# A fused retention and bilinear FFN kernel: two loads moved behind a group's transposing DMAs, and one early stretch of attention work moved eight products later

## The chip, the cores and the metric

The kernel runs on one core of one Trainium2 chip. The metric is device time in microseconds (us); the kernel before has a median of 329.77 us in three runs (328.47 to 330.15).

## What is computed

q, k and v are float32 of shape (8 batches, 8 heads, 576 positions, 64). Cut to what matters:

```python
scores = matmul(q, k.transpose(0, 1, 3, 2)) / sqrt(64)
Dmat   = where(i >= j, gamma[h] ** (i - j), 0)        # gamma[h] = 1 - 2 ** (-5 - h)
attn   = matmul(scores * Dmat, v)                     # no softmax
x      = attn.transpose(0, 2, 1, 3).reshape(4608, 512)
out    = ((x @ w_a) * (x @ w_b)) @ w_out              # 512 -> 1536 -> 512, float32 out
```

Because the mask is a power of a distance and there is no softmax, attention can be done block by block: a block of 64 positions takes the scores inside itself, and everything earlier through a running 64x64 sum of k times v, the state.

## The kernel before

**FFN.** The 4608 tokens go through the FFN in ten blocks of 512, 256, 256 and then seven times 512 tokens. In a block, w_a and w_b are taken in 12 chunks of 128 columns: four products `pa` (TensorE, summed in PSUM), a cast `ha` by ScalarE, four products `pb`, and a multiplication `hT` by VectorE. Then for every 128 tokens twelve products `po` give an output tile, which ScalarE (even tiles) or VectorE (odd tiles) copies to `osb` and SyncE's queue (SP) stores. All of these products are issued at line 466. They share a PSUM pool of four buffers.

**Attention.** The tokens come in 18 groups of 256, numbered from 0. Groups 0 to 2 are made ahead of the others, in six steps. Each group n from 3 on goes through:

1. `load_pair(n)` (L148): six loads by SP of 256 KB each, two for each of q, k, v, into float32 tiles with four buffers for each of the three.
2. `ahead(n)` (L481 to L486): POOL casts q and k to `qkb` in six instructions and scales v to `vb` in one.
3. `turn(n)` (L514): two transposing DMAs by SP, `qkb` to `qkT`, q first and then k.
4. `stretch(n, n - 1)`: 128 small matmuls on TensorE, in four sets of 32: the outputs of group n - 1 from the states (L638), the new sums of group n (L548), the scores of group n (L610), the outputs of group n - 1 from the keys (L651). Group 5's outputs are not in a stretch: `open_alone(5)` does the first set and `close_outputs(5)` the last.
5. What follows for VectorE and ScalarE (adding sums, casting states, masking scores, scaling the output into the FFN's input `xT`) is put in a list `later`. FFN code takes one piece of it at certain points, in a 256-token block once after each chunk and at three places and the end of an output tile.

**Order of the work.** A list `todo`, written by hand, holds (position, function, arguments). The position counts products of the FFN (512 columns wide; one of 256 columns counts a half). The FFN generator runs through its blocks and, at the end of a chunk or of every fourth `po`, runs what is due. Each engine executes its own instructions in the order in which they are issued, so the list sets the order on every engine's queue, on SP's and POOL's too. Around the change: block 2 (tokens 768 to 1023) lies at positions 216 to 288, its `po` from 264; block 3 at 288 to 432, block 4 at 432 to 576. `load_pair(9)` and `load_pair(10)` stand at 345.1 and 345.2, `ahead(9)` at 390, `turn(9)` at 422, stretch (9, 8) at 460, `ahead(10)` at 462, `turn(10)` at 494, stretch (10, 9) at 532. `turn(n)` for n from 9 on ends with `load_pair(n + 2)`. SP runs well behind these positions in the first half of the kernel, since the transfers are slower than the list.

**Early waits.** From group 6 on, `wait_early` makes FFN products ahead of a stretch wait for what the stretch needs: the seventh before it for the scaled v, the sixth for the transposed q, the third for the transposed k (L468 to L472).

**Buffers that bind around the change.** `qkb`, `vb` and `qkT` have three buffers each, the sums and states two, the PSUM tiles for scores and for outputs one. A stretch of its own block takes two of the four FFN buffers for `kv` until VectorE has added both halves.

Of the kernel before, what the change touches and what calls it, by code (L numbers as in the profile page):

```python
# [18 lines left out]
def kernel(  # L19
# [44 lines left out]
    def rows_of(n):  # L64

        if n not in LEFT:
            b, m = PAIRS[n]
            return [(kp, 0, 128, b, 256 * m + 128 * kp) for kp in (0, 1)]
        return [(i // 2, 64 * (i % 2), 64, 4 * LEFT[n] + i, S - 64)
                for i in range(4)]  # L70
# [69 lines left out]
    def load_pair(n, which=(0, 1, 2)):  # L140
        if n >= NP:
            return
        paired.setdefault(n, {})
        for i in which:
            name, src = (("qf", q), ("kf", k), ("vf", v))[i]
            t = stage.tile([128, 2 * DM], FP32, tag=name, name=name + "2")
            for kp, r0, m, b, s0 in rows_of(n):
                nc.sync.dma_start(  # L148
                    t[r0:r0 + m, kp * DM:(kp + 1) * DM]
                    .rearrange("p (h d) -> p h d", h=H),  # L150
                    src[b, :, s0:s0 + m, :].rearrange("h s d -> s h d"))
            paired[n][i] = t
# [13 lines left out]
    Q, K, V = 0, 1, 2  # L166
# [342 lines left out]
    def turn(n):  # L509
        qkb = of(natural, n)[0]  # L510
        qkT = qkt_pool.tile([128, 2, 2, HP, 128], BF16, tag="qkT",
                            name="qkT2")
        for w in (0, 1):
            ready[n].append(nc.sync.dma_start_transpose(  # L514
                qkT[:, w].rearrange("p k c s -> p (k c) s"), qkb[:, w]))
        transposed[FIRST + n, "pair"] = qkT
        if n >= 9:
            load_pair(n + 2)

    def of(store, n):  # L520
        return store[FIRST + n, "pair"]
# [402 lines left out]
    def turn_step(i):  # L924
# [3 lines left out]
    todo = [(100, early_casts, ()), (112, turn_step, (4,)),  # L928
            (112.1, cast_step, (5, Q, "act")), (116, score_step, (4,)), (116, state_step, (4,)),
            (124, turn_step, (5,)), (128, output_step, (4,)),  # L930
            (128, score_step, (5,)), (128, state_step, (5,)),
            (140, output_step, (5,))]
# [1 line left out]
    todo += [(136, total_of, (2,))]  # L934
    todo += [(28 + 6 * step, pair_tables, (step,)) for step in range(13)]
    todo += [(170, stretch, (3, None)), (197, stretch, (4, 3)),
             (232, stretch, (5, 4)), (266, open_alone, (5,)),
             (270, close_outputs, (5,)), (336, stretch, (6, None)),
             (372, stretch, (7, 6)), (408, stretch, (8, 7))]
    for n in range(8, NP, 2):  # L940
        todo += [(starts[n] - 116, stretch, (n + 1, n)),
# [4 lines left out]
    placed = {args[0]: at for at, fn, args in todo if fn is stretch}  # L946
    casts = {3: 116, 4: 116, 5: 141, 6: 200, 7: 250, 8: 330}
    turns = {4: 116, 5: 145, 6: 240, 7: 338, 8: 345}
    loads = {7: 212, 8: 271, 9: 345.1, 10: 345.2}
    todo += [(145.1, load_pair, (6, (K,))),  # L950
             (145.2, load_pair, (6, (Q,))), (145.3, load_pair, (6, (V,)))]
    for n in range(9, NP):
        casts[n], turns[n] = placed[n] - 70, placed[n] - 38
# [1 line left out]
    for fn, places in ((ahead, casts), (turn, turns), (load_pair, loads)):  # L955
        todo += [(at, fn, (n,)) for n, at in places.items()]
# [45 lines left out]
```

## Time and profile before

| | us |
|---|---|
| median of three runs | 329.77 (328.47 to 330.15) |
| the profiled execution | 332.06 |
| its span, first to last instruction | 330.3 |
| TensorE busy in the span | 322.0 |
| VectorE, ScalarE, POOL busy | 161.9, 129.2, 116.6 |
| mean granted TensorE clock | 0.995 |
| bytes moved | 50.37 MB, 152 GB/s over the span |
| stretch (5, 4) on TensorE | 73.97 to 75.50 |
| outputs of group 5: opened, closed | 84.17, 85.52 |
| first product of block 3 | 89.36 |
| stretches (7, 6), (8, 7), (9, 8), (10, 9) begin | 109.19, 117.44, 133.34, 150.48 |

An entry of a timeline gives start and length in us, the engine, the line and the operation, the tiles (out<-in), the shape, the count of instructions merged, and in brackets how long the engine sat idle before it and what ended that. PE is TensorE's matmul queue, PEld its weight loads, SPq SyncE's DMA issues: an issue's length is the time that SP spends on it, and the data lands later. The first half of the kernel also brings in the weights and most of q, k and v.

### The profile page before, as it was taken

Reading aid. Unit: us, or ns where it says so; the run is one execution under the profiler, and the core shown is the slowest. Engines: PE = TensorE matmul, PEld = TensorE weight load, DVE = VectorE, ACT = ScalarE, POOL = GpSimd, SP = SyncE. Lnnn points to the kernel's source line nnn. Section 1 sums busy time; section 2 is a strip of 40 time slices with the busy share of each in tenths; the row PEclk is TensorE's granted clock in tenths of the full one; section 3 lists DMA queues with packets and bytes.
Section 4 is the critical chain, followed back from the end, with each engine's and each line's share of the span. In section 5 each row is a group of like instructions: output and inputs, shape, how many; then the busy total and the mean of one; then the engine's idle time right before and its main releaser. Section 6 shows DMA issues by size and latency. Waiting matters only on the chain.

```text
span 330.3 us, 8653 instructions
## 1 busy us (share of the span) xinstructions
PE 322.0 (97%) x3615; PEld 166.3 (50%) x3615; DVE 161.9 (49%) x289; ACT 129.2 (39%) x286; POOL 116.6 (35%) x150
## 2 busy tenths in 40 slices
PE   7899999999999997999999999999999999999996
PEld 3564458778444553545454545454445444444443
DVE  5744454667246753656165625662456246414321
ACT  6745754464335532343235312532332333213321
POOL 3890068640957086554063405360420000000000
PEclk9999999999999999799999999999999999999999
DMA  7999999999999999991699158945850420031013
GB/s 218 250 175 207 251 234 212 204 188 211 226 223 213 203 197 227 232 223 52 158 209 223 50 133 191 214 84 147 180 113 2 136 58 0 2 95 32 3 25 102
DMA packets 143175, 50.37 MB, mean 152 GB/s; under 512 B 124576, under 2 KB 138656, under 8 KB 143136
## 3 DMA queue, kind: packets, MB, share of 16 engines
q1 hardware_dynamic: 138384, 45.10, 65.3%
q0 software_dynamic: 4752, 4.72, 8.9%
q8 instruction: 28, 0.46, 0.6%
q14 instruction: 11, 0.09, 0.1%
HBM read 37.75 MB, written 9.44 MB: 143 GB/s over the span
## 4 chain that ended last, share of the span: by engine, by line
PE 78%; SPq 9%; DMA 8%; POOL 2%; issue 1%; ACT 1%; DVE 0%; POOLq 0%; ACTq 0%; DVEq 0%
PE po L466 24%; PE pb L466 24%; PE pa L466 23%; SPq L148 5%; DMA vf<-in_v_dram 5%; SPq L159 2%; DMA qf<-in_q_dram 2%; PE o L638 1%; PE o L651 1%; DMA qkT<-qkb 1%; POOL qkb L485 1%; PE sc L610 1%; PE kv L548 1%; SPq L514 1%; PE pa L738 1%
## 5 line engine op out<-in xcount | busy, mean ns | idle before, releaser
L779 DVE TENSOR_TENSOR hT<-ha,pb 128x512 bf16<-128x512 bf16 (+1 forms) x120 | 75.7, 633 | 101.7 <-PE pb L466 94.9
L768 ACT CAST ha<-pa 128x512 bf16<-128x512 f32 (+1 forms) x120 | 64.6, 542 | 121.9 <-PE pa L466 118.7
L466 PE MATMUL pb<-xT,wb_sb 128*128 128x512 bf16 (+1 forms) x480 | 111.8, 358 | 0.2
L466 PE MATMUL pa<-xT,wa_sb 128*128 128x512 bf16 (+1 forms) x468 | 109.5, 359 | 1.8 <-DMA qkT<-qkb 1.8
L466 PE MATMUL po<-wo_sb,hT 128*128 128x512 bf16 (+2 forms) x444 | 97.5, 374 | 0.0
L466 PEld LDWEIGHTS <-wb_sb 128*128 128x128 bf16 x480 | 46.9, 98 | 47.0 <-DMA qkT<-qkb 0.8
L466 PEld LDWEIGHTS <-wa_sb 128*128 128x128 bf16 x468 | 44.9, 98 | 46.7 <-DMA qkT<-qkb 2.3
L466 PEld LDWEIGHTS <-hT 128*128 128x128 bf16 x444 | 41.9, 98 | 47.3
L481 POOL CAST qkb<-qf 64x1024 bf16<-64x1024 f32 x15 | 15.5, 1030 | 85.0 <-DMA qf<-in_q_dram 72.9
L486 POOL TENSOR_TENSOR vb<-vf,vs 128x1024 bf16<-128x1024 f32 x15 | 28.5, 1902 | 12.6 <-PE o L651 4.4
L804 DVE COPY osb<-po 128x512 f32<-128x512 f32 (+1 forms) x16 | 10.9, 683 | 39.6 <-PE po L466 39.6
L802 ACT COPY osb<-po 128x512 f32<-128x512 f32 (+1 forms) x21 | 12.0, 569 | 45.5 <-PE po L466 45.5
L661 DVE TENSOR_TENSOR xT<-o,qs 128x512 bf16<-128x512 f32 x30 | 19.5, 683 | 5.0 <-PE o L651 5.0
L573 DVE TENSOR_TENSOR sums<-kv,sums 128x256 f32<-128x256 f32 x44 | 18.6, 424 | 3.0 <-PE kv L548 1.0
L619 DVE TENSOR_TENSOR sT<-sc,mask 128x512 bf16<-128x512 f32 x30 | 19.5, 682 | 0.0
L485 POOL CAST qkb<-kf 64x512 bf16<-64x512 f32 x30 | 17.6, 614 | 0.7
L485 POOL CAST qkb<-qf 64x512 bf16<-64x512 f32 x30 | 17.6, 614 | 0.6
L481 POOL CAST qkb<-kf 64x1024 bf16<-64x1024 f32 x15 | 15.8, 1052 | 4.3 <-DMA kf<-in_k_dram 3.5
L577 ACT CAST states<-sums 64x512 bf16<-64x512 f32 x26 | 16.0, 617 | 0.3
L678 ACT COPY fence<-o 128x2 f32<-128x2 f32 x15 | 2.4, 160 | 17.5 <-PE o L638 17.5
L310 POOL CAST qkb<-kf 128x512 bf16<-128x512 f32 x5 | 3.1, 614 | 16.6 <-DMA kf<-in_k_dram 16.6
L820 PE MATMUL w<-ones 128*128 128x512 bf16 x19 | 7.4, 509 | 1.5 <-DVE idxp_f L203 1.5
(87 smaller groups left out, 166.4 us busy)
## 6 DMA issues: line engine op xcount, KB each, us to landing
qf<-in_q_dram SPq DMA_DIRECT2D x32, 256.0 KB, 4.9
kf<-in_k_dram SPq DMA_DIRECT2D x32, 256.0 KB, 5.2
vf<-in_v_dram SPq DMA_DIRECT2D x32, 256.0 KB, 5.1
out_dram<-osb SPq DMA_DIRECT2D x25, 256.0 KB, 2.2
out_dram<-osb SPq DMA_DIRECT2D x20, 128.0 KB, 2.5
wo_sb<-in_moe_w_out_dram POOLq DMA_DIRECT2D x3, 512.0 KB, 16.0
qf<-in_q_dram SPq DMA_DIRECT2D x8, 128.0 KB, 3.3
kf<-in_k_dram SPq DMA_DIRECT2D x8, 128.0 KB, 3.5
```

The source lines that it names most:

```text
L148: nc.sync.dma_start(t[r0:r0 + m, kp * DM:(kp + 1) * DM] .rearrange("p (h d) -> p h d", h=H), src[b, :, s0:s0 + m, :].rearrange("h s d -> s ...
L466: products.append(nc.tensor.matmul(out, lhsT, rhs, **kw))
L481: nc.gpsimd.tensor_copy(qkb[0:64, w], t[0:64])
L485: nc.gpsimd.tensor_copy(to[:, :, 1 - r], fro[:, :, r])
L486: scaled = nc.gpsimd.tensor_tensor(vb.rearrange("p (k h d) -> p k h d", k=2, h=H), vf.rearrange("p (k h d) -> p k h d", k=2, h=H), vs2[:, ...
L573: nc.vector.tensor_tensor(sums[:, i], own, prev, op=ALU.add)
L577: nc.scalar.copy(to(half(1 - r)), fro(half(r)))
L619: nc.vector.tensor_tensor(sT[:, on].rearrange("p c k s -> p (c k) s"), sc[:, on].rearrange("p c k s -> p (c k) s"), mask3.unsqueeze(1).to_ ...
L661: nc.vector.tensor_tensor(x_of(t0, 128).rearrange("p c (a s) -> p c a s", a=2), o[:, :, :, kp].rearrange("p a c s -> p c a s"), qs[:, :, s ...
L768: nc.scalar.copy(ha[:, 0:n], pa[:, 0:n])
L779: nc.vector.tensor_tensor(hT[:, F, 0:n], has[F][:, 0:n], pb[:, 0:n], op=ALU.mult)
L802: nc.scalar.copy(osb[:, cols], po[:, 0:width])
```

## The change

The loads of group 10 at position 345.2 keep only q. Its k and v are loaded from `turn(9)`, after the two transposing DMAs of group 9 and ahead of the loads of group 11. In block 2, stretch (5, 4) goes from position 232 to 240, the opening of group 5's outputs from 266 to 272 (done at the edges 268 and 272) and their closing from 270 to 276 (done at 272 and 276). Nothing is computed otherwise, and no instruction is added.

```diff
@@ turn(n)
         transposed[FIRST + n, "pair"] = qkT
+        if n == 9:
+            load_pair(n + 1, (K, V))
         if n >= 9:
             load_pair(n + 2)
@@ todo
     todo += [(170, stretch, (3, None)), (197, stretch, (4, 3)),
-             (232, stretch, (5, 4)), (266, open_alone, (5,)),
-             (270, close_outputs, (5,)), (336, stretch, (6, None)),
+             (240, stretch, (5, 4)), (272, open_alone, (5,)),
+             (276, close_outputs, (5,)), (336, stretch, (6, None)),
              (372, stretch, (7, 6)), (408, stretch, (8, 7))]
...
-    loads = {7: 212, 8: 271, 9: 345.1, 10: 345.2}
-    todo += [(145.1, load_pair, (6, (K,))),
+    loads = {7: 212, 8: 271, 9: 345.1}
+    todo += [(345.2, load_pair, (10, (Q,))),
+             (145.1, load_pair, (6, (K,))),
              (145.2, load_pair, (6, (Q,))), (145.3, load_pair, (6, (V,)))]
```

## The prediction

> **What bounds the kernel now.** The page comes first: who is busy, and where the exceptions are.
>
> ```profile
> PE 322.0 (97%) x3615; PEld 166.3 (50%) x3615; DVE 161.9 (49%) x289; ACT 129.2 (39%) x286; POOL 116.6 (35%) x150
> ...
> PEclk9999999999999999799999999999999999999999
> DMA  7999999999999999991699158945850420031013
> ```
>
> TensorE is busy 97% of 330.3 us: only time in which it waits or runs slowly can be won. In 40 slices of 8.26 us the granted clock falls once, in slice 16 (132 to 140 us). The DMA engines are full in slices 1 to 17 and then go slack: the first 148 us are paced by transfers, the rest by TensorE. The waits of TensorE's two queues name the place; columns are us in total, times, longest:
>
> ```profile
> PEld L466 <- DMA qkT<-qkb: 3.1, 3, 2.3
> PE pa L466 <- DMA qkT<-qkb: 1.8, 1, 1.8
> ```
>
> Every long wait for data past the first 50 us is for the transposed q and k. By windows, 2.9 of the 3.1 us lie between 128 and 134 us and 0.2 between 105 and 112 us. TensorE's timeline at that place (start, us, form, count, idle before):
>
> ```profile
> 128.20 1.03 PE L466 MATMUL pb<-xT,wb_sb 128*128 128x512 bf16 x4
> 129.06 0.59 PE L466 MATMUL pa<-xT,wa_sb 128*128 128x512 bf16 x2
> 131.47 0.60 PE L466 MATMUL pa<-xT,wa_sb 128*128 128x512 bf16 x2 [1.82 <-DMA qkT<-qkb]
> 131.92 1.49 PE L466 MATMUL pb<-xT,wb_sb 128*128 128x512 bf16 x4
> ...
> 135.18 1.55 PE L466 MATMUL pa<-xT,wa_sb 128*128 128x512 bf16 x4
> 136.57 1.03 PE L466 MATMUL pb<-xT,wb_sb 128*128 128x512 bf16 x4
> ```
>
> This is the stretch of groups (9, 8), whose early waits (L468) sit 6 and 3 products ahead of it. The price: a set of four products starts 0.865 us after the one before it, pb to stretch takes 0.95 us (108.24 to 109.19, at the stretch (7, 6)), a stretch 1.24 us (109.19 to 110.43). So from 129.06 to 136.57 there should be 0.865 + 0.95 + 1.24 + 0.865 = 3.92 us; there are 7.51. **Lost: 3.59 us**, of it 2.00 in pa, 0.47 in pb, 0.60 in the stretch, 0.52 in the next pa. The last two wait for nobody; they run at half clock, as three windows say (PE busy, PEld, DVE, ACT, POOL, PEclk, DMA share, GB/s):
>
> ```profile
> 129.60:133.00 3.40, 1.50 (x7) 0.42 (x6) 0.42 (x1) 0.58 (x1) 0.86 (x1) 0.98 0.93 197
> 132.85:136.30 3.45, 3.45 (x125) 2.21 (x124) 2.38 (x5) 0.16 (x1) 0.46 (x1) 0.51 1.31 235
> 137.00:148.00 11.00, 11.00 (x52) 5.00 (x51) 6.43 (x10) 5.71 (x11) 7.06 (x9) 1.00 1.16 226
> ```
>
> Why is the transposed data late? POOL's cast of group 9's k ended at 119.4, its v at 121.4. The DMAs were issued 5.6 us later, by SP's timeline:
>
> ```profile
> 108.97 1.27 SPq L148 DMA_DIRECT2D qf<-in_q_dram  x2
> 110.28 3.30 SPq L148 DMA_DIRECT2D kf<-in_k_dram  x2
> 113.63 1.78 SPq L148 DMA_DIRECT2D vf<-in_v_dram  x2
> 115.46 2.19 SPq L148 DMA_DIRECT2D qf<-in_q_dram  x2
> 117.69 3.81 SPq L148 DMA_DIRECT2D kf<-in_k_dram  x2
> 121.54 1.75 SPq L148 DMA_DIRECT2D vf<-in_v_dram  x2
> 123.38 3.50 SPq L719 DMA_DIRECT2D out_dram<-osb  x3
> 126.99 3.29 SPq L514 DMA_TRANSPOSE qkT<-qkb  x2
> 130.33 1.20 SPq L148 DMA_DIRECT2D qf<-in_q_dram  x2
> ```
>
> Lines 1 to 3 are group 9's loads, 4 to 6 group 10's, then three stores, then group 9's transposes (landed at 131.43 and 132.33 by the trace's landing marks), then group 11's loads. SP takes them in program order. Group 10's k and v, 5.6 us of issuing and 1 MB, stand ahead of something needed sooner.
>
> **Part one: loads of k and v of group 10 behind the transposes of 9.** No instruction is added or removed; four load DMAs pass three stores and two transposes on SP's queue. SP is done with group 10's q at 117.65. The first two stores' rows are ready by then or nearly (copies end at 115.5 and 118.2); the third's copy ends at 122.1 (ACT, 121.49 + 0.58), so the third store, 0.35 us to issue, goes at about 122.1 and the transposes at 122.5 and 123.8. Where the engines have little queued, a transpose lands 3.35 us after issue (group 11: 159.90 to 163.25; 161.27 to 164.64). So: 125.9 and 127.2. TensorE asks for them at 129.5 and 130.1. Margin 2.9 to 3.6 us; worst, at the 5.7 us that the page of these tiles gives as their longest landing, 128.2 and 129.5, still in time. **Gain 3.59 us.**
>
> What is late next? K and v of 10 are issued from 125.1, group 11's loads behind them. The first load lands some 3.6 us after issue (162.61 to 166.19), the others 1.1 to 1.2 us apart, as under load in this trace: 10's at 128.7, 129.9, 131.1, 132.2, 11's to 139.2 (before: 140.2). POOL casts 10's k by 132.5 (1.03 + 1.17 us), its v by 134.2 (1.90 us); SP reaches group 10's transposes at about 137 (before 138.11). Landing: about 142 (before 141.86 and 142.78). The stretch (10, 9) starts at 150.48 now and, 3.59 earlier, at 146.9; its waits stand at 145.5 and 146.1. Margin 3.4 us, where it was 6. Group 11's transposes (159.90) follow the stores of the next block, which follow TensorE, so they move with it. After 148 us the transfers have room, and the gain reaches the end.
>
> **The clock's share.** The half clock costs 0.60 + 0.52 and part of pb's 0.47. The row: one wait of 1.82 us and a shorter one, and then 3.41 us at half clock. [...] The row is this case's; I take it.
>
> **Part two: stretch (5, 4) at 240, outputs of group 5 opened at 272 and closed at 276.** The same 128 small matmuls stand two chunks of d_ff later (a chunk is here 4 products of pa and 4 of pb, 256 wide, 0.87 us): 1.74 us. Outputs close one edge of four products later: 0.86 us. SP's and POOL's orders stay the same. The trace has the stretch at 73.97 to 75.50. Behind it 0.6 us are lost: six sets, 75.50 to 78.74, 3.24 us, should take 2.62. kv holds two of four PSUM buffers until DVE's sums, so the products alternate with ACT and DVE in the other two. That comes with the stretch; I cost it the same. Six deferred pieces then fall on chunks 6 to 11 instead of 4 to 9. The last, ACT's swapped states, now ends at 82.91 (81.66 + 1.25) and would end at about 84.65; group 5's outputs open at 84.17 and would at about 84.9. Cover 0.25 us, where it was 1.26. The closing part reads masked scores that end at 82.82, later at 84.6, against 86.3. DVE's scaling (86.10 to 87.39) moves to about 88.2, ahead of the next block's first product at 89.36. **Value 0**; bounds -0.6 (the loss behind the stretch vanishes, as if DVE were free) and +0.9 (that edge's 0.86 us no longer hidden). A gain here ends at the 0.2 us wait before the stretch (7, 6), whose transposes landed at 108.27, just when wanted.
>
> **Sum.** -3.59 + 0 = -3.6. The profiled execution took 332.06 us, 330.3 of span and 1.8 around it: it becomes 328.5, span 326.7. It lies 2.3 us above the median of 329.77 (runs 328.47 to 330.15). Taken off the median: **326.2 us**, 1.1% faster.
>
> **Rivals.**
> (a) *Less to win without the profiler.* The profiled execution is 2.3 us slower than the median, and the loss turns on a meeting of two streams: transposes landing 2 us sooner against TensorE leave no wait and no half clock. If all 2.3 us are this stall, 3.6 - 2.3 = 1.3 us remain: 328.5. For it: the lowest run, 328.47, is what the profiled one would be without the stall. Against: the profiler may cost its 2.3 us elsewhere.
> (b) *The transposes stay late*, since the third store, tied to TensorE's own third output tile, holds SP. Decided at SP past 126. The copy at 122.1 speaks against it. Time: 329.8.
> (c) *Slower: group 10 becomes late.* If k and v of 10 land late, cast, transposes and the stretch (10, 9) follow. With the transposes landing at 145.5 the margin is gone; each us after that is a us lost, and a wait of 2 us brings the half clock's 1.5 us again. The gain is eaten at a wait of about 2.1 us (147.6, five us behind the 142.78 of before: all of 10's k and v in front, nothing saved behind). At 150 it costs 4.5 + 1.5 - 3.6 = 2.4 us: 332.2. For it: 3.4 us of margin instead of 6, and transfer engines that stand nearly idle from 122.5 to 126. Against: the bytes before these transposes are the same as before.
>
> **Chances.** Forecast 0.64. (a) 0.19; (b) 0.06; (c) 0.11. A measurement of this kernel tells about 0.5%, 1.65 us, from no change. Faster: the forecast and 0.02 of (a), 0.66. Same: the rest of (a) and (b), 0.23. Slower: 0.11. Range: 325.0 (part two's -0.6, and 0.6 for a half clock whose 3.41 us cost their full half, 1.7, where 1.12 were seen) to 330.2 ((a) and (b) with the scatter of the runs shown); (c) and a little below are left out. The forecast's own range is 325.0 to 327.6.
>
> **What would show it.** Right: no wait of pa or its weight loads for qkT near 129, no 7 in the clock's row, SP issuing 9's transposes near 122.5, 10's landing before 145. Part two right: the block that begins at token 1024 still has its first product at 89.4 us. Wrong: a wait before the stretch (10, 9) (rival c), transposes still issued past 126 (b), a clean profile with an unchanged median (a), or ACT's conversion ending after 85 with TensorE idle.

## The result, and the profile after

The changed kernel took 327.82 us (median of 6 runs, 327.51 to 328.26) against 329.83 us (328.47 to 330.3): a ratio of 0.9944, 95% interval 0.9925 to 0.9964, 0.6% faster where 1.1% was forecast. Its profiled execution took 327.93 us with a span of 326.2, where 328.5 and 326.7 were forecast. So the profiled execution came out 0.6 us below its forecast and 4.1 us shorter than before, and the median fell by half of that, 2.0 us.

SP's timeline of the changed kernel (start, us, line, operation, tiles, count; lines past 518 stand two lower in this file than in the one before):

```profile
115.43 2.10 SPq L148 DMA_DIRECT2D qf<-in_q_dram  x2
117.63 4.26 SPq L721 DMA_DIRECT2D out_dram<-osb  x3
122.00 3.72 SPq L514 DMA_TRANSPOSE qkT<-qkb  x2
125.77 1.24 SPq L148 DMA_DIRECT2D kf<-in_k_dram  x2
127.05 1.96 SPq L148 DMA_DIRECT2D vf<-in_v_dram  x2
129.06 2.30 SPq L148 DMA_DIRECT2D qf<-in_q_dram  x2
...
138.38 2.85 SPq L514 DMA_TRANSPOSE qkT<-qkb  x2
```

Group 9's transposes are issued at 122.00 instead of 126.99 and landed at 126.36 and 127.66. Group 10's k and v follow them; group 10's transposes go at 138.38 (138.11 before) and landed at 142.20 and 143.41. TensorE's timeline at the old place of the stall, and two windows there (us, PE busy, PEld, DVE, ACT, POOL, clock, DMA share, GB/s):

```profile
128.52 1.03 PE L466 MATMUL pa<-xT,wa_sb 128*128 128x512 bf16 x3
129.38 1.03 PE L466 MATMUL pb<-xT,wb_sb 128*128 128x512 bf16 x4
...
131.80 0.81 PE L466 MATMUL pa<-xT,wa_sb 128*128 128x512 bf16 x3 [0.16 <-issue]
```

```profile
129.60:133.00 3.40, 3.24 (x130) 2.08 (x130) 2.30 (x5) 1.08 (x3) 2.21 (x3) 1.00 1.34 225
132.85:136.30 3.45, 3.45 (x17) 1.55 (x16) 2.85 (x6) 2.27 (x5) 1.93 (x2) 1.00 1.23 214
```

No wait for qkT is left before stretch (9, 8), and the clock is full there; 0.3 us of TensorE's weight loads waiting for qkT remains before stretch (7, 6), where it was 0.2. Stretch (9, 8) begins at 130.34 instead of 133.34, stretch (10, 9) at 146.35 instead of 150.48. Block 3 begins at 88.82 instead of 89.36.

### The profile page after: what moved, and what is told of

Read it like the earlier page. It is cut to its first block, busy times and chain, and to the rows that moved or that the text cites. A ratio compares the mean times of both kernels' runs of the same rounds, so it can differ in the third digit from the quotient of the medians.

```text
span 326.2 us, 8616 instructions
## 1 busy us (share of the span) xinstructions
PE 315.3 (97%) x3576; PEld 165.0 (51%) x3615; DVE 161.7 (50%) x289; ACT 129.4 (40%) x286; POOL 116.5 (36%) x150
## 4 chain that ended last, share of the span: by engine, by line
PE 92%; SPq 2%; DMA 2%; issue 1%; ACT 1%; DVE 0%; ACTq 0%; DVEq 0%
PE pb L466 29%; PE po L466 28%; PE pa L466 27%; SPq L159 2%; DMA qf<-in_q_dram 2%; PE o L640 2%; PE o L653 2%; PE sc L612 1%; PE kv L550 1%; PE pa L740 1%; PE o L426 0%; ACT vb L318 0%; PE tp L327 0%; PE tp L505 0%; DVE hT L781 0%
## 5 line engine op out<-in xcount | busy, mean ns | idle before, releaser
L466 PE MATMUL pa<-xT,wa_sb 128*128 128x512 bf16 (+1 forms) x452 | 106.8, 356 | 1.4 <-issue 1.0
L466 PE MATMUL po<-wo_sb,hT 128*128 128x512 bf16 (+2 forms) x429 | 94.8, 373 | 1.7 <-issue 1.4
L350 DVE TENSOR_TENSOR sT<-sc,mask_s 128x1024 bf16<-128x1024 f32 x6 | 7.3, 1221 | 1.7 <-PE sc L342 1.7
```

The costliest lines, as they stand in the source:

```text
L466: products.append(nc.tensor.matmul(out, lhsT, rhs, **kw))
```

## The experiments

**Four kernels on one chip: the kernel before again, each part alone, both.** First the kernel before, not edited:

> The kernel before, unchanged, executed again. Theory A (the loss of 3.59 us before stretch (9, 8) is the same in every execution, and the profiled one was slower by 2.2 us elsewhere): its new profile shows the wait of about 2 us and the half clock, and its runs all have a mean granted clock near 0.995. Theory B (the stall or its half clock differs from execution to execution): the wait or the half clock is smaller or gone in the new profile, and the runs' clocks spread between 0.995 and 1.0, the slower runs at the lower clock. Time 329.8 by both, ratio 1.000.

Measured: 329.02 us (12 runs, 327.88 to 331.83), ratio 1.0001 (0.9972 to 1.0030). The new profiled execution took 327.88 us, the fastest of the twelve, and the stall is not in it:

```profile
119.22 2.65 SPq L148 DMA_DIRECT2D vf<-in_v_dram  x2
121.98 2.65 SPq L719 DMA_DIRECT2D out_dram<-osb  x3
124.73 2.75 SPq L514 DMA_TRANSPOSE qkT<-qkb  x2
```

```profile
128.48 1.03 PE L466 MATMUL pa<-xT,wa_sb 128*128 128x512 bf16 x3
129.34 1.03 PE L466 MATMUL pb<-xT,wb_sb 128*128 128x512 bf16 x4
```

The program is the same. From the first load of group 9 to its transposes SP needed 16.5 us here (108.25 to 124.73) and 18.0 us in the first profile (108.97 to 126.99); between 100 and 125 us the DMA engines moved 224 GB/s here and 206 there. The transposes landed at 128.42 and 129.48. The first is 3.0 us sooner than in the first profile: 0.7 because the loads began earlier, 1.5 on SP's queue, 0.8 between issue and landing. Of the 2.9 us for which weight loads waited before stretch (9, 8), 0.3 remained. Theory B held for the stall. It missed in part: the slowest run of the 12 has a clock of 1.0, and all but one of the 12 are at 1.0.

Part one alone:

```diff
+        if n == 9:
+            load_pair(n + 1, (K, V))
...
-    loads = {7: 212, 8: 271, 9: 345.1, 10: 345.2}
+    loads = {7: 212, 8: 271, 9: 345.1}
+    todo += [(345.2, load_pair, (10, (Q,))),
```

> Only group 10's k and v behind group 9's transposes; stretch (5, 4) as before. Theory A (part one makes the whole gain): ratio 0.994, 327.9 us, no wait for qkT before stretch (9, 8). Theory B (part one gains 3.6 us as in the profile and part two takes some 1.7 us back): 326.2 us, ratio 0.989.

Measured: 328.03 us (12 runs), ratio 0.9962 (0.9934 to 0.9990), no wait for qkT. Eleven of the 12 runs lie between 327.45 and 328.51, the twelfth at 330.46.

Part two alone:

```diff
-             (232, stretch, (5, 4)), (266, open_alone, (5,)),
-             (270, close_outputs, (5,)), (336, stretch, (6, None)),
+             (240, stretch, (5, 4)), (272, open_alone, (5,)),
+             (276, close_outputs, (5,)), (336, stretch, (6, None)),
```

> Only stretch (5, 4) 8 products and group 5's outputs 6 later; the loads as before. Theory A (part two is worth nothing, since the wait before stretch (9, 8) comes afterwards and swallows any small shift): 329.8 us, ratio within 0.2% of 1. Theory B (part two costs): 331.5 us, ratio 1.005. If it removes the 0.3 us by which stretch (5, 4) was long in the profile before, that time shows up as a longer wait for qkT.

Measured: 329.44 us, ratio 1.0009 (0.9978 to 1.0039). In its profile pa waits 0.63 us before stretch (9, 8), where it waited 1.82 in the first profile, with the transposes landing at 129.74 and 130.66 and the clock full: the same stall in a third size.

Both parts again:

> Both parts again, on the same chip as the other three. Theory A: like part one alone, ratio 0.994. Theory B (part two takes back): slower than part one alone by 1.7 us.

Measured: 328.03 us, ratio 0.9972 (0.9943 to 1.0001, which just takes in no change), the median of part one alone. Part one makes the gain; part two neither adds nor takes anything that can be measured. This set's kernel before had a median of 328.76 us.

**The dose.** If the place of group 9's transposes on SP's queue sets the time, more loads ahead of them must cost more. With two more:

```diff
         if n >= 9:
-            load_pair(n + 2)
+            load_pair(n + 2, (K, V) if n == 9 else (Q, K, V))
...
+    todo += [(345.3, load_pair, (11, (Q,))),
```

> The kernel before, with one more pair of loads (q of group 11) ahead of group 9's transposes. Theory A (the place of these transposes on SP's queue sets the time): they are issued and land 2.3 us later (two loads at 1.15 us each), every run waits some 2 to 4 us before stretch (9, 8); 1.0 to 1.5 us more where the clock halves: ratio 1.007 to 1.012, 331.2 to 332.8 us. [...] Theory B (the wait is covered by something else, and the chip's transfers alone make the spread): ratio within 0.3% of 1.

With six more:

```diff
-        if n >= 9:
+        if n >= 10:
             load_pair(n + 2)
...
+    todo += [(345.3, load_pair, (11,)),
```

> The kernel before, with all six loads of group 11 ahead of group 9's transposes. Theory A: transposes 6.9 us later, a wait of 6 to 9 us before stretch (9, 8) and half clock in every run: ratio 1.021 to 1.027, 336 to 338 us, clock 0.995 or lower. What comes later is moved by the same time and nothing is won back. Theory B: ratio within 0.5% of 1.

Measured: two more, 331.04 us, ratio 1.0075 (1.0047 to 1.0103); six more, 338.63 us, ratio 1.0295 (1.0263 to 1.0326), a little over its expected range. TensorE's line behind the wait and the window after it, first with two more loads, then with six:

```profile
132.32 0.61 PE L466 MATMUL pa<-xT,wa_sb 128*128 128x512 bf16 x2 [2.51 <-DMA qkT<-qkb]
```

```profile
132.30:136.00 3.70, 3.33 (x129) 1.91 (x130) 1.45 (x3) 0.75 (x2) 0.00 (x0) 1.00 1.06 215
```

```profile
136.59 1.03 PE L466 MATMUL pa<-xT,wa_sb 128*128 128x512 bf16 x2 [6.53 <-DMA qkT<-qkb]
```

```profile
136.50:141.70 5.20, 5.12 (x128) 2.67 (x129) 1.90 (x4) 0.75 (x2) 0.39 (x1) 0.50 0.99 217
```

The dose works. The clock is the surprise: an idle time of 2.51 us, longer than the first profile's 1.82, is followed by full clock, and one of the eight runs with two loads is below 0.998 (0.994). With 6.53 us the clock is halved in the profile, and all four runs have a mean clock of 0.985 to 0.990.

The length of a gap alone does not decide in these profiles. In the first one the granted clock is full up to 132.85 us, half for 3.41 us and full again from 136.26 on; with six more loads the half clock lasts 6.83 us. Here are windows with the columns as above (the clock is the third number from the end): the 3.42 us ahead of the half clock of the first profile and the half clock itself, then two windows of that length with two more loads.

```profile
129.43:132.85 3.42, 1.52 (x8) 0.42 (x6) 0.59 (x1) 0.58 (x1) 1.03 (x1) 1.00 0.88 187
132.85:136.26 3.41, 3.41 (x125) 2.21 (x124) 2.34 (x5) 0.16 (x1) 0.42 (x1) 0.50 1.29 232
```

```profile
128.12:131.53 3.41, 1.69 (x8) 0.59 (x6) 1.01 (x2) 0.59 (x1) 3.37 (x4) 1.00 1.08 295
131.53:134.95 3.42, 2.28 (x84) 1.14 (x87) 0.53 (x1) 0.75 (x2) 0.31 (x1) 1.00 1.05 220
```

In the first profile TensorE is busy for 1.52 of the 3.42 us ahead of the half clock (44%). With two more loads the longer wait is split between two windows, busy for 49% and 67%, and the clock is full in both. With six, there is no product at all from 131.44 to 134.85, and the clock is half from then to 141.7 (a mean of 0.87 from 130.00 to 136.50, 0.50 up to 141.70, 1.00 behind it). What decides whether a gap is followed by half clock is not shown: no edit moved a gap of one length to another moment.

**The price of the half clock.** The same six loads, and products of ones where TensorE would idle:

```diff
+    todo += [(456, warm, (28, 512))]
     todo.sort(key=lambda e: e[0])
```

> The kernel with all six loads of group 11 ahead of group 9's transposes, and 28 products of ones (128x512, 0.216 us each, 6.0 us, results unused) in the eight products' place just ahead of the early waits of stretch (9, 8): TensorE works where it stood idle for 6.5 us. Theory A (half clock is part of the price of a long wait): the waiting time is the same, the half clock is gone or shorter; 2 to 3 us less than without the products: 335.6 to 336.6 us, clock 1.0. Theory B (only the wait costs): unchanged, 338.6 us.

Measured: 336.08 us, ratio 1.0202 (1.0165 to 1.0240). The window of the transposes' wait and the one after it:

```profile
130.00:136.50 6.50, 5.91 (x27) 2.37 (x25) 0.00 (x0) 0.13 (x1) 2.74 (x4) 1.00 1.12 285
136.50:141.70 5.20, 4.91 (x137) 2.86 (x138) 3.24 (x7) 1.36 (x4) 1.90 (x1) 1.00 0.99 207
```

Work of no use, put where TensorE waits, makes the kernel 2.6 us faster than without it. The two kernels ran in different sets on different chips, but their ratios to the kernel before of their own set, 1.0202 and 1.0295, have intervals that lie apart. A measure of the stall itself is the time from the first score product of stretch (8, 7) to that of (10, 9) in each profile:

| kernel | us | over 29.45 | half clock there |
|---|---|---|---|
| changed; before again | 29.45; 29.45 | 0 | no |
| part two alone | 30.31 | 0.86 | no |
| two more loads | 32.66 | 3.21 | no |
| before, first profile | 33.04 | 3.59 | 3.41 us |
| six more loads | 38.30 | 8.85 | 6.83 us |
| six more, kept busy | 36.65 | 7.20 | no |

The last two rows differ by 1.65 us; their transposes landed within 0.2 us of each other, counted from stretch (8, 7), so about 1.5 us of it, by the author's estimate from these two figures, is the clock. The rest of the 2.6 us lies ahead of stretch (8, 7), which began 1.0 us later in the profile without the products.

**The margin of group 10.** All of group 10's loads behind group 9's transposes:

```diff
         if n == 9:
-            load_pair(n + 1, (K, V))
+            load_pair(n + 1)
...
-    todo += [(345.2, load_pair, (10, (Q,))),
```

> The changed kernel, with q of group 10 too behind group 9's transposes. Theory A (the margin before stretch (10, 9) is 2 to 3.5 us, and group 9's transposes are tied to the third store, so they gain nothing): transposes of 9 still issued at 122, transposes of 10 some 2.3 us later, landing at 144.5 to 146 against 145.0 and 145.7 asked: a wait of 0 to 1 us, 328.0 to 329.0 us, ratio to before 0.997 to 1.000. Theory C (group 10 is already on the edge in the changed kernel): a wait of over 2 us and half clock, 330.5 us or more.

Measured: 328.5 us, ratio 0.9989 (0.9965 to 1.0014). Group 9's transposes are issued at 121.87, as before this edit; the third store holds them there. Group 10's landed at 144.24 and 145.31, 1.9 us later than in the changed kernel, just when they are wanted; the profile shows 0.2 us of waiting. Three of ten runs took 330.2 to 330.6, where one of the changed kernel's eleven in the next set was over 329. This fits theory A; that those three waited there is argued, since no profile of them exists.

**The next edges.** Group 7's transposes ahead of the v loads of group 8, in the changed kernel:

```diff
-    turns = {4: 116, 5: 145, 6: 240, 7: 338, 8: 345}
+    turns = {4: 116, 5: 145, 6: 240, 7: 271.1, 8: 345}
...
+             (271, load_pair, (8, (Q, K))), (271.2, load_pair, (8, (V,))),
```

> The changed kernel, with group 7's transposes ahead of the v loads of group 8. Theory A (stretch (7, 6) is the next edge: its transposes land at 107.8 to 108.0 when asked for at 108.0, so that a slow execution waits there): they land near 102, and the median falls by up to 0.4 us against the changed kernel, 327.5 to 327.8 us, with no run over 329. Theory B (nothing is left to win from transfers): as the changed kernel, 328.0 us. Group 8's own transposes may come 1 us later, with 5 us of margin.

Measured: 328.26 us (327.36 to 329.58), ratio 0.9970 (0.9945 to 0.9996). No wait for qkT is left, but no gain is seen, and three of the 12 runs are over 329, where theory A expected none. Another wait showed up near 71 us (us in total, times, longest):

```profile
ACT osb L804 <- DMA out_dram<-osb: 1.2, 1, 1.2
PE pb L466 <- ACT osb L804: 1.1, 1, 1.1
```

An output tile waits for one of the four `osb` buffers, whose store stands behind the loads of group 5's v on SP. The edit, at position 271, comes later than this and did not make the wait; the profile with two more loads has 0.4 us of it too. So two more kernels: those loads behind that store, without and with the edit above.

```diff
-             (116, load_pair, (5, (V,))), (145, store_held, ())]
+             (120, load_pair, (5, (V,))), (145, store_held, ())]
```

> The changed kernel, with the loads of v of group 5 behind the store of the first block's second output tile instead of ahead of it. One profile shows ScalarE waiting 1.24 us for that tile's buffer near 71 us and TensorE 1.11 us for ScalarE; in the other profiles the store lands at 70.6 to 70.8, at about the time when ScalarE asks. Theory A (this is the next edge): the store lands 1 to 2 us earlier, no wait near 71 us in any execution, median 0.2 to 0.4 us under the changed kernel's. Theory B (later waits swallow it, or TensorE paces all): as the changed kernel within 0.1%.

> As the kernel before this one, with group 7's transposes also ahead of the v loads of group 8. Theory A (both edges matter, each in some executions): a median of 327.4 to 327.6 us and no run over 328.5. Theory B: as the changed kernel, 328.0 us.

> The changed kernel, on the same chip as the other three: 327.8 to 328.1 us, ratio 0.994 to 0.997. The spread of the kernel before is what moves the ratio from one set of runs to another; the changed kernel's own median should stay within 0.3 us of its two earlier ones (327.82 and 328.03).

Measured on the same chip: 327.47 us (7 runs), ratio 0.9951 (0.9923 to 0.9979); with both edits 327.95 us (12 runs), 0.9957 (0.9934 to 0.9980); the changed kernel 328.18 us (11 runs), 0.9969 (0.9942 to 0.9995). With both edits the median is above the range of theory A, and three runs are over 328.5, up to 330.07. The store-first profile has the shortest span of all, 325.4 us, and its weight loads wait 0.2 us in all for qkT after 50 us. The changed kernel's third profile does wait before stretch (7, 6), whose transposes landed at 108.84 in it:

```profile
PEld L466 <- DMA qkT<-qkb: 1.1, 2, 0.6
```

Both waits do occur, each in some profiles. That either edit beats the changed kernel is not shown: the intervals overlap.

## Why the prediction was right, and where it was not

- **What bounds the kernel, and why the transposes are late:** right. Moving four loads takes the wait away; two and six more loads make it longer (pa waits 2.51 and 6.53 us where it waited 1.82).
- **Part one, the times:** issue at 122.5 forecast, 122.00 measured; landing 125.9 and 127.2 forecast, 126.36 and 127.66 measured; group 10's landing about 142 forecast, 142.2 and 143.4 measured; stretch (10, 9) at 146.9 forecast, 146.35 measured. The third store does set the issue: in seven of the eight profiles with this order the transposes go 0.46 or 0.47 us after the copy of that output tile ended (1.58 in the eighth), where the order before has 3.24 to 9.84. The margin before stretch (10, 9) is smaller than forecast, 2 to 3 us where 3.4 were, since TensorE came 0.5 us sooner and the second transpose landed at 143.4.
- **Part two, value 0:** right. The half microsecond by which block 3 began earlier is 0.23 already at the start of block 2; the rest is the 0.3 us by which stretch (5, 4) was long in the first profile (1.53 us). At the old position it takes 1.25 to 1.68 us in six profiles, at the new one 1.25 or 1.26 in all eight: a few tenths at most, which no median shows. ACT's swapped states ended at 84.22, before the outputs opened at 84.50: the thin cover held. What part two guards against is small: the scores of group 5 waited 0.2 and 0.3 us for their transposes in two of the six profiles with the old position (two and six more loads), and in none of the eight with the new one.
- **The clock's share failed:** "The row is this case's; I take it." Of 97 executions of the kernel before in the experiments, 8 have a mean clock of 0.995 or less (329.89 to 332.34 us); the others are at 0.998 or more. The first profile, at 0.995, was such an execution; the row was right for it and wrong for most others. With two more loads, a gap of 2.51 us in the profile, seven of eight runs kept a clock of 0.999 or more (the eighth had 0.994), and with six, a gap of 6.53 us, none did (0.985 to 0.990). The length of the gap sets no bound in these profiles: 1.82 us was followed by 3.41 us of half clock, and 2.51 us by none.
- **The sum failed in its size:** "Taken off the median: 326.2 us". 3.59 us is what one execution lost. The profiles of the old order lose 3.59, 0.86 and 0 at this place, and their executions took 332.06, 329.07 and 327.88 us. In the later sets together the kernel before has a median of 329.04 us and quartiles of 328.60 and 329.69 (97 runs); the changed one, over all its sets, has 328.03, 327.81 and 328.26 (29 runs). The old order reaches the changed kernel's 328.03 in 8 of its 97 runs. The change removes a spread; what it is worth depends on where in that spread the median lies: 0.9944, 0.9972 and 0.9969 in three sets. The first set was lucky for the forecast: its kernel before, at 329.83, lay above the upper quartile of the later runs; by these medians the gain is about 1.0 us and not 2.0. Even so 327.82 lies just outside the forecast's own range (325.0 to 327.6), and inside the wide one only because that takes in rivals (a) and (b). Rival (a) said this, with 328.5 us and a chance of 0.19, and its evidence was on the table: the profiled execution lay 1.9 us above the slowest of the runs shown. The profiler, which (a) also names, does not explain the slow first profile: the second profiled execution of the same kernel was the fastest of its twelve.
- **Rivals (b) and (c):** fell. Group 10 was in time, with 2 us to spare; it takes two more loads to use them up.

Open: two of the 29 runs of the changed kernel took 331.5 us at a clock of 0.995. No profile shows where they waited; group 7's transposes are the nearest suspect. And nine of the 97 runs of the kernel before took 330.0 to 331.8 us at a clock of 0.999 or more. A wait without half clock, as with two more loads, would fit, but none of them was profiled.

## What to carry to other kernels

A queue that executes in order is a schedule: put what is needed soonest ahead of what is needed later, and price the move by the issue times that it skips. Before a stall of one profile is subtracted from a median, look where the profiled execution lies among the runs; if it lies above all of them, its stall is an upper end, and a second profile of the same kernel is worth more than any reading of the first. Where two streams meet with a margin near zero, expect a spread and not a loss, and expect the next meeting with no margin to take over the rest of it.

## What the runs showed of the hardware

The same 12 loads and 3 stores took SP 16.5 us in one execution of a program and 18.0 in another; with what else shifted, the transposes behind them landed 3.0 us sooner, and a stall of 3.6 us was gone. At this stall a halved clock came in pieces of 3.41 us (first profile, after an idle time of 1.82 us) and of 6.83 us (six more loads, begun within an idle time of 6.53 us), and none came with an idle time of 2.51 us (two more loads). 28 useless products in a wait of 6.5 us left no half clock (1.00 from 136.50 to 141.70, where it was 0.50) and, by the author's estimate from a difference of 1.65 us, saved about 1.5 us.
